# A cross-read with a GELU layer on one core: one sum, two bank copies and the state's transposes change places

## The chip, the cores and the metric

The kernel runs on one core of a Trainium2 chip. TensorE multiplies, VectorE and ScalarE do elementwise work and are the only ones that empty PSUM here, GpSimd (POOL) copies between SBUF tiles and issues loads, SyncE (SP) issues the stores and the transposing DMAs. Each engine works through its own queue strictly in order. The metric is the device time of one launch in microseconds; three runs of the kernel before gave a median of 205.29 us (205.24 to 205.36).

## The reference

`x` is 8 batches by 8 heads by 512 rows of 64 numbers, `state` the same with 32 rows instead of 512. For every batch and head:

```python
a = softmax(x @ state.T / 8);   xread = a @ state      # 512 rows read the state
a2 = softmax(state @ x.T / 8);  sread = a2 @ x         # 32 rows read x
rows = concatenate(xread, sread)                        # 544 rows per batch and head
out = gelu(rows_of_all_heads(512) @ w_in) @ w_out       # 512 -> 2048 -> 512
```

The heads of a row are laid side by side (8 x 64 = 512 columns), so the second part works on 8 x 544 = 4352 rows.

## The kernel before, in words

**Staging.** A batch's 512 rows of x are one *turn* b; the 256 state rows of all batches are collected in `XSR` and put through both weights during the last turn. The work on `xread` is folded: for each batch `P = blockdiag(state) @ w_in` (256 by 2048, `p_mm`, lines 423 to 436, in four *chunks* of 512 columns, each with two PSUM banks t = 0 and 1) takes the place of `w_in`, so that a hidden chunk is `gelu(P.T @ a.T)`: `M` (lines 489 to 501) makes hidden chunk m of 128 columns with two matmuls of 512 columns (`hp`), and ScalarE's Gelu (line 501) writes `g`. Sixteen chunks make a batch.

**The second product.** `g @ w_out` is computed per batch as a 2 x 2 block product with seven block products in place of eight, `X(b, name)` (line 621) with names 3, 4, 5, 1, 2, 7, 6: 16 matmuls each, into four fixed PSUM banks `o0` to `o3` (3 and 5 share `o0`, 4 and 2 `o1`, 1 and 7 `o2`, 6 has `o3`). Five of them need a sum of two quadrants of `g`, which VectorE makes just ahead: `g_sum(b, name)` (line 582, 128 x 2048 bf16, tile `gsum`, three buffers). Sum "6" is quadrant (1, 0) minus (0, 0), so it needs the hidden chunks 0 to 7; sum "5" needs all sixteen. Results are combined on VectorE (lines 618, 640, 652, 654) and GpSimd (lines 610, 646), and stored by SP (line 605). Line 618 is the output addition behind product "2", which first needs GpSimd's `v`; line 654 is the one behind product "7", which empties bank `o2`.

**The loop.** Turn 0 and most of turn 1 are a separate run-up. The loop at line 1153 runs b = 2 to 7, each over eight *block pairs* p = 0 to 7; each pair makes two hidden chunks of batch b (`M(k, k + 1)`) and, mostly, one block product. For b < 7 and nb = b + 1:

- p = 0: sum 5 and product 4 of batch b - 1, sum 1; a load of x and its re-layout on GpSimd (`rearr`, line 225). For b = 2 also chunk 2 of P of batch 2 (`pmat(2, 2)`)
- p = 1: scores and Exp of batch nb; product 5, sum 2
- p = 2, 3: the two halves of the normalization of batch nb (`norm`, lines 353 to 356); product 1 and sum 7 in p = 2; in p = 3 sum "6" of batch b, product 2 of batch b - 1, and for b = 2 also chunk 3 of P (`pmat(2, 3)`)
- p = 4: two hidden chunks alone
- p = 5: the transposing DMA of a (`atr_dma`, SP's queue); product 7 of batch b - 1; then `p_all`; `rearr_ones` on GpSimd (line 235); product 3 of batch b
- p = 6: two hidden chunks (12 and 13)
- p = 7: `srt(b)`, hidden chunks 14 and 15, product 6 of batch b

**p_all** (line 929) first does the state's read of batch b (`reads_mm`: matmuls of line 905 into one PSUM tile, copied out by ScalarE in line 913 as `sraw`), then the four chunks of P for batch nb, then the eight bank copies (`p_copy`: ScalarE t = 0, VectorE t = 1), then `reads_norm` on VectorE (lines 921, 922), which leaves the normalized read `srm`. In turn 6 it reads batches 6 and 7 together. The eight banks of P come from the fixed `o0`, `o1`, `o3`, `o2` (chunk 0 bank 0, chunk 2 banks 0 and 1, chunk 3 bank 0) and from a pool of four rotating banks `f` (the other four), which `hp`, the state's read and the transposes `srT` share. So the fourth chunk needs line 654 to have emptied `o2`, product 3 needs ScalarE's copy out of `o0`, and product 6 needs `o3` and sum "6".

**srt** (line 413) transposes `srm` on TensorE into a tile of the pool `f` and has VectorE copy it into `XSR`, where the batch is the innermost index (a stride of eight numbers). In turn 6 it is called twice, with two tiles.

The order on every queue is the order of these calls: the tile framework runs with a manual schedule and adds only the semaphores.

Of the kernel before, what the change touches and what calls it, by code (L numbers as in the profile page):

```python
# [10 lines left out]
BF16 = mybir.dt.bfloat16  # L11
# [6 lines left out]
def kernel(  # L18
# [8 lines left out]
    nc = tc.nc  # L27

    B, H, S, D = x.shape
    _, _, NS, _ = state.shape  # L30
# [3 lines left out]
    HC = H // 2  # L34
# [33 lines left out]
    ident = persist.tile([128, 128], BF16, name="ident")  # L68
# [161 lines left out]
    def rearr_ones(b):  # L230
        A = atts[b]
        eng = nc.vector if b < 2 else nc.gpsimd
        src = xbs[b].rearrange("p (t c) (j d) -> p t c j d", t=2, d=D)
        for t in range(2):
            eng.tensor_copy(  # L235
                out=A.xo[:, :, :, 2 + 64 * t:66 + 64 * t].rearrange("p j c d -> p c j d"),
                in_=src[:, t],
            )
# [174 lines left out]
    def srt(b):  # L413
        A = atts[b]
        ps = ps_f.tile([128, HC, NS], BF16, name="srT", tag="f")
        nc.tensor.transpose(  # L416
            ps.rearrange("p c n -> p (c n)"), A.srm.rearrange("q t d -> q (t d)"), ident
        )
        nc.vector.tensor_copy(out=XSR[:, :, :, b], in_=ps)  # L419

    Ps = {}

    def p_mm(b, f, tiles):
        if b not in Ps:
            Ps[b] = att.tile([128, 2, d_ff], BF16, name="P", tag="P")
        ps = [tiles([128, 512], "p_ps") for t in range(2)]
        for c in range(HC):
            for t in range(2):
                nc.tensor.matmul(  # L429
                    ps[t][32 * c:32 * c + 32, :],  # L430
                    lhsT=sbd[64 * t:64 * t + 64, b, c, 32 * t:32 * t + 32],
                    rhs=w_in_bf[64 * t:64 * t + 64, c, f * 512:(f + 1) * 512],
                    start=True,
                    stop=True,
                )
        return ps

    def p_copy(b, f, ps):
        dst = Ps[b][:, :, f * 512:(f + 1) * 512]
        nc.scalar.copy(out=dst[:, 0, :], in_=ps[0])  # L440
        nc.vector.tensor_copy(out=dst[:, 1, :], in_=ps[1])  # L441

    def pmat(b, f):
        p_copy(b, f, p_mm(b, f, ftile))
# [137 lines left out]
    def g_sum(b, name):  # L582
        (h0, k0), (h1, k1), op = G_SUMS[name]
        t = apool.tile([128, MH, 256], BF16, name="gsum", tag="gsum")
        nc.vector.tensor_tensor(out=t, in0=g_q(b, h0, k0), in1=g_q(b, h1, k1), op=op)  # L585
        xs[b, "g" + name] = t
# [34 lines left out]
    def X(b, name):  # L621
        bank = {"3": 0, "4": 1, "5": 0, "2": 1, "1": 2, "6": 3, "7": 2}[name]
        first = name in "3416"
        if first:
            xs[b, bank] = otile([128, 2, NH], "xp", bank)
        ps = xs[b, bank]
        lhs = {"3": (0, 0), "4": (1, 1)}.get(name)
        lhs = xs[b, "g" + name] if lhs is None else g_q(b, *lhs)
        rhs = {"5": w_q[1][1], "2": w_q[0][0]}.get(name)
        rhs = w_sum[name] if rhs is None else rhs  # L630
        x_mm(ps, lhs, rhs, first)
        if name == "3":
            xs[b, "s3"] = c_tile("s3")
            if b > 1:
                nc.scalar.copy(out=xs[b, "s3"], in_=ps)
            for h in range(2):
                xs[b, "o", h] = hpool.tile([128, 2, d_model], FP32, name="oh", tag=f"oh{h}")
        elif name == "4":
            xs[b, "s34"] = c_tile("s34")
            nc.vector.tensor_tensor(out=xs[b, "s34"], in0=ps, in1=xs[b, "s3"], op=ALU.add)  # L640
        elif name == "5":
            o = xs[b, "o", 0][:, :, NH:]
            nc.scalar.copy(out=o, in_=ps)  # L643
            xs[b, "u"] = c_tile("u")
            x_out(b, 0, right)
            nc.gpsimd.tensor_tensor(out=xs[b, "u"], in0=xs[b, "s34"], in1=o, op=ALU.subtract)  # L646
        elif name == "2":
            nc.scalar.copy(out=xs[b, "o", 1][:, :, :NH], in_=ps)  # L648
            c22(b)
        elif name == "1":  # L650
            xs[b, "q"] = c_tile("q")
            nc.vector.tensor_tensor(out=xs[b, "q"], in0=ps, in1=xs[b, "s34"], op=ALU.add)  # L652
        elif name == "7":
            nc.vector.tensor_tensor(  # L654
                out=xs[b, "o", 0][:, :, :NH], in0=ps, in1=xs[b, "u"], op=ALU.add
            )
            x_out(b, 0, left)
# [258 lines left out]
    def reads_norm(bs, raw):  # L916
        for i, b in enumerate(bs):
            A = atts[b]
            A.srm = att.tile([128, 2, D], BF16, name="srm", tag="srm")
            inv = att.tile([128, 2], FP32, name="inv", tag="inv")  # L920
            nc.vector.reciprocal(out=inv, in_=raw[:, i, 0:130:129])
            nc.vector.tensor_tensor(
                out=A.srm,
                in0=raw[:, i, 1:129].rearrange("q (t d) -> q t d", t=2),
                in1=inv[:, :].to_broadcast((128, 2, D)),
                op=ALU.mult,
            )

    def p_all(b, bs):
        raw = reads_mm(bs)  # L930
        done = []
        for f, at in enumerate(((0, None), (None, None), (1, 3), (2, None))):
            it = iter(at)

            def tiles(shape, name):
                i = next(it)
                return ftile(shape, name) if i is None else otile(shape, name, i)

            done.append((b, f, p_mm(b, f, tiles)))
        for x in done:  # L940
            p_copy(*x)
        reads_norm(bs, raw)

    def p_copy_v(b, f, ps):
        for t in range(2):
# [207 lines left out]
    for b in range(2, B):  # L1153
        nb = b + 1
        for p in range(8):
            k = 16 * b + 2 * p
            if p == 1 and nb < B:
                scores(nb, 0)
                scores(nb, 1)
            if p in (2, 3) and nb < B:  # L1160
                norm(nb, p - 2)
            if p == 3 and nb + 1 < B:
                xtr_dma(nb + 1)
            if p == 5 and nb < B:
                atr_dma(nb)
            if p == 7 and nb < B:
                srt(b)
                if nb == B - 1:
                    srt(nb)
            if nb == B and p < 5:  # L1170
                read_out_slot(p)
                if p == 4:
                    r_homes()
                    r_sum("5")
                    r_sum("2")
                continue
            M(k, k + 1)
            if b == 2 and p in (0, 3):
                pmat(2, 2 + p // 3)
            if b == 2 and p == 1:  # L1180
                w_sums(4)
            if p < 4 or (p == 4 and nb == B):
                if p == 0:
                    g_sum(b - 1, "5")
                    if b > 2:
                        sr_w("5216"[b - 3])
                if p == 3:
                    g_sum(b, "6")
                X(b - 1, "45127"[p])
                if p < 3:  # L1190
                    g_sum(b - 1, "127"[p])
            if p == 0 and b + 3 < B:
                hold_for(b, 0)
                load_x(4 if b == 2 else b + 3)
            if p == 6 and b == 2:
                hold_for(b, 12)
                load_x(5)
            if p == 0 and nb + 1 < B:
                begin(nb + 1)
                rearr(nb + 1)  # L1200
            if nb == B:
                if p == 5:
                    g_sum(b, "6")
                    R("3")
                    r_sum("1")
                    R("4")
                    r_sum("6")
                    r_sum("7")
                if p == 6:
                    R("5")  # L1210
                    X(b, "3")
                    R("2")
                    R("1")
                if p == 7:
                    R("6")
                    X(b, "6")
                continue
            if p == 5:
                X(b - 1, "7")
                reads = (b, nb) if nb == B - 1 else (b,)  # L1220
                p_all(nb, reads)
                if b == 2:
                    rearr_ones(3)
                elif nb + 1 < B:
                    rearr_ones(nb + 1)
                X(b, "3")
            if p == 7:
                if b == 2:
                    rearr_ones(4)
                X(b, "6")  # L1230
    b = B - 1
    for name in "521":
# [39 lines left out]
```

## Time and profile before

| what | us |
|---|---|
| median of three runs | 205.29 |
| profiled execution | 205.13 |
| its span | 203.2 |
| TensorE busy (matmuls) | 196.0 (96%) |
| VectorE busy | 162.9 (80%) |
| ScalarE busy | 136.6 (67%) |
| GpSimd busy | 68.4 (34%) |
| sums `gsum` on VectorE, 35 | 50.2, mean 1.449, median 1.218, longest 3.166 |
| bank copies of P by line 441 on VectorE, 29 | 18.3, mean 0.681 |
| bank copies of P by line 440 on ScalarE, 29 | 15.3, mean 0.597 |
| copies into `XSR`, 8 | 5.7, mean 0.758 |
| granted TensorE clock | full throughout |

A line of the timeline reads: start, duration, engine, line of the kernel, operation, tile written and tiles read, shapes, number of instructions merged, and in brackets how long the engine stood idle before it and what released it. Durations of neighbours on one engine overlap by up to a tenth of a microsecond, so a row of four copies of 0.67 takes 2.48. PE is TensorE, PEld its weight loads, DVE VectorE, ACT ScalarE. Matmuls are pipelined: a busy TensorE need not be one at its peak, so lost time on it is read from the distance between the starts of two matmuls against the usual one (0.22 us for a matmul of 512 columns).

### The profile page before, as it was taken

To read this page: it belongs to the slowest core of one execution; us is meant where nothing else is said; L and a number is where in the kernel's file an instruction comes from. 1 tells how busy PE (TensorE), PEld (TensorE's weight loads), DVE (VectorE), ACT (ScalarE), POOL (GpSimd) and SP (SyncE) were. 2 spreads that over 40 slices of the span, in tenths; PEclk is the share of its full clock that TensorE was granted. 3 is DMA by queue.
4 is the path that set the end of the run, shared out by engine and by line. 5 is a ranking of instruction groups with operands and counts; after the bars stand their busy time and mean duration, and the time that the engine had idled before them with its cause. 6 is when DMAs were issued, how large, how long until landed. Compare 5 with 4: busy or idle time off the path is not lost.

```text
span 203.2 us, 4901 instructions
## 1 busy us (share of the span) xinstructions
PE 196.0 (96%) x2030; PEld 133.9 (66%) x2035; DVE 162.9 (80%) x255; ACT 136.6 (67%) x245; POOL 68.4 (34%) x75
## 2 busy tenths in 40 slices
PE   7899999999999999999999999999999999999993
PEld 2434544466766687666776677677776887878893
DVE  2954876789999889996899777967799888895882
ACT  3785678798985779656967597687857576864120
POOL 8972503324259297430527302420220002200000
PEclk9999999999999999999999999999999999999999
DMA  6999999986655879633772508270107001040134
GB/s 192 199 172 203 206 198 197 185 163 126 89 104 106 206 87 143 135 126 84 94 167 77 133 0 127 39 205 0 52 3 206 3 0 55 0 158 0 52 107 155
DMA packets 40566, 23.16 MB, mean 114 GB/s; under 512 B 21856, under 2 KB 39136, under 8 KB 40544
## 3 DMA queue, kind: packets, MB, share of 16 engines
q0 software_dynamic: 13984, 8.10, 29.3%
q1 hardware_dynamic: 25872, 14.36, 27.7%
q10 hardware_dynamic: 688, 0.39, 0.6%
q8 instruction: 16, 0.26, 0.5%
q14 instruction: 6, 0.05, 0.1%
HBM read 17.30 MB, written 8.91 MB: 129 GB/s over the span
## 4 chain that ended last, share of the span: by engine, by line
PE 68%; DVE 15%; DMA 5%; POOL 4%; issue 4%; ACT 2%; DVEq 0%; POOLq 0%; ACTq 0%
PE xp L591 30%; PE hp L494 20%; DVE gsum L585 6%; DMA xb<-in_x_dram 5%; PE op L536 3%; PE sp L798 3%; PE rp L864 3%; POOL w_in_bf L105 2%; DVE P L441 2%; DVE a L356 2%; PE op L520 2%; PE xp L703 2%; PE p_ps L429 2%; DVE cs L353 1%; PE pt L333 1%
## 5 line engine op out<-in xcount | busy, mean ns | idle before, releaser
L501 ACT ACTIVATE g<-hp 128x512 bf16<-128x512 f32 x124 | 66.3, 606 | 21.5 <-PE hp L494 17.0
L494 PE MATMUL hp<-AT,P 128*128 128x512 bf16 x248 | 62.0, 379 | 0.6 <-DVE P L441 0.4
L591 PEld LDWEIGHTS <-gsum 128*128 128x128 bf16 x528 | 51.4, 98 | 11.4 <-DVE q L652 0.2
L585 DVE TENSOR_TENSOR gsum<-g 128x2048 bf16<-128x2048 bf16 x35 | 50.2, 1449 | 4.1 <-ACT g L501 4.0
L494 PEld LDWEIGHTS <-P 128*128 128x128 bf16 x248 | 23.2, 98 | 21.1 <-issue 2.2
L591 PE MATMUL xp<-ws,gsum 128*128 128x256 bf16 x304 | 36.3, 273 | 0.0
L591 PE MATMUL xp<-ws,g 128*128 128x256 bf16 x224 | 26.8, 273 | 0.2
L591 PE MATMUL xp<-w_out_bf,gsum 128*128 128x256 bf16 x224 | 26.6, 273 | 0.0
L591 PEld LDWEIGHTS <-g 128*128 128x128 bf16 x224 | 21.5, 98 | 5.0 <-issue 1.6
L646 POOL TENSOR_TENSOR u<-s,oh 128x512 f32<-128x512 f32 x6 | 8.8, 1467 | 40.6 <-ACT oh L643 40.6
L225 POOL COPY x<-xb 128x1024 bf16<-128x1024 bf16 x12 | 14.3, 1225 | 16.6 <-DMA xb<-in_x_dram 16.6
L441 DVE CAST P<-p_ps 128x512 bf16<-128x512 f32 x29 | 18.3, 681 | 1.2 <-PE p_ps L429 1.0
L440 ACT CAST P<-p_ps 128x512 bf16<-128x512 f32 x29 | 15.3, 597 | 4.8 <-PE p_ps L429 4.7
L235 POOL COPY xo<-xb 128x1024 bf16<-128x1024 bf16 x12 | 13.2, 1129 | 5.0 <-PE sr L905 5.0
L610 POOL TENSOR_TENSOR v<-q,oh 128x512 f32<-128x512 f32 x6 | 8.2, 1371 | 19.6 <-ACT oh L648 17.2
L356 DVE TENSOR_TENSOR a<-e,ics 128x512 bf16<-128x512 bf16 x14 | 11.7, 833 | 0.5
L536 PE MATMUL op<-w_out_bf,g 128*128 128x512 bf16 x44 | 11.1, 380 | 0.5 <-issue 0.3
L353 DVE TENSOR_REDUCE cs<-e 128x16 f32<-128x512 bf16 x14 | 9.5, 677 | 0.7 <-ACT e L340 0.7
L429 PE MATMUL p_ps<-w_in_bf,sbd 64*32 64x512 bf16 x248 | 9.6, 381 | 0.3 <-DVE oh L654 0.3
L501 ACT ACT_TABLE_LOAD x7 | 9.0, 1283 | 0.1
L419 DVE COPY XSR<-srT 128x128 bf16<-128x128 bf16 x8 | 5.7, 758 | 3.8 <-PE srT L416 3.8
L536 PEld LDWEIGHTS <-g 128*128 128x128 bf16 x48 | 4.1, 97 | 5.9 <-issue 1.1
(137 smaller groups left out, 233.2 us busy)
## 6 DMA issues: line engine op xcount, KB each, us to landing
out_dram<-oh SPq DMA_DIRECT2D x15, 256.0 KB, 2.7
xb<-in_x_dram POOLq DMA_DIRECT2D x7, 512.0 KB, 7.5
out_dram<-oh SPq DMA_DIRECT2D x6, 512.0 KB, 2.8
w_in_bf<-in_moe_w_in_dram POOLq DMA_DIRECT2D x6, 256.0 KB, 11.8
out_dram<-osb SPq DMA_DIRECT2D x5, 256.0 KB, 3.2
w_out_bf<-in_moe_w_out_dram POOLq DMA_DIRECT2D x4, 256.0 KB, 8.0
w_out_bf<-in_moe_w_out_dram POOLq DMA_DIRECT2D x2, 512.0 KB, 13.3
x0f<-in_x_dram SPq DMA_DIRECT2D x3, 256.0 KB, 3.8
```

The lines of the kernel that those rows point to most:

```text
L225: nc.gpsimd.tensor_copy(out=A.x4[:, :, :, 64 * t:64 * t + 64].rearrange("p j c d -> p c j d"), in_=src[:, t],)
L235: eng.tensor_copy(out=A.xo[:, :, :, 2 + 64 * t:66 + 64 * t].rearrange("p j c d -> p c j d"), in_=src[:, t],)
L353: nc.vector.reduce_sum(out=cs, in_=e4, axis=AX.X)
L356: nc.vector.tensor_tensor(out=A.a[:, :, hs].rearrange("p g (c n) -> p g c n", n=NS), in0=e4, in1=ics[:, :, :].to_broadcast((128, G, 2, NS) ...
L429: nc.tensor.matmul(ps[t][32 * c:32 * c + 32, :], lhsT=sbd[64 * t:64 * t + 64, b, c, 32 * t:32 * t + 32], rhs=w_in_bf[64 * t:64 * t + 64, c ...
L440: nc.scalar.copy(out=dst[:, 0, :], in_=ps[0])
L441: nc.vector.tensor_copy(out=dst[:, 1, :], in_=ps[1])
L494: nc.tensor.matmul(hp, lhsT=Ps[b][:, t, m * 128:(m + 1) * 128], rhs=atts[b].AT[:, :, t, :], start=(t == 0), stop=(t == 1),)
L501: nc.scalar.activation(out=gs[b][:, m, :], in_=hp, func=AF.Gelu)
L536: nc.tensor.matmul(ops[b, j], lhsT=gs[b][:, m, j * 128:(j + 1) * 128], rhs=w_out_bf[:, m, :], start=(m == 0), stop=(m == MC - 1),)
L585: nc.vector.tensor_tensor(out=t, in0=g_q(b, h0, k0), in1=g_q(b, h1, k1), op=op)
L591: nc.tensor.matmul(ps[:, j - js[0], :], lhsT=lhs[:, m, 128 * j:128 * j + 128], rhs=rhs[:, m, :], start=(first and j == js[0] and m == 0), ...
```

## The change

Three edits, all inside turns 2 to 6:

- Sum "6" of batch b leaves block pair 3 and is made behind `p_all` in block pair 5, so it stands on VectorE's queue behind the bank copies and `reads_norm`, and no longer ahead of lines 618 and 654.
- In `p_all` ScalarE copies both banks of chunk 0 (five copies instead of four; VectorE three instead of four). In turn 2, block pair 3, ScalarE copies both banks of chunk 3 of batch 2.
- The transposes of `srm` stand behind hidden chunks 14 and 15 instead of ahead of them, and those of turn 6 share one PSUM tile and leave it in one VectorE copy.

The queues of GpSimd and SP keep their order.

```diff
+    def srts(bs):
+        ps = ps_f.tile([128, len(bs), HC, NS], BF16, name="srT", tag="f")
+        for i, b in enumerate(bs):
+            nc.tensor.transpose(
+                ps[:, i].rearrange("p c n -> p (c n)"),
+                atts[b].srm.rearrange("q t d -> q (t d)"),
+                ident,
+            )
+        nc.vector.tensor_copy(
+            out=XSR[:, :, :, bs[0]:bs[-1] + 1], in_=ps.rearrange("p b c n -> p c n b")
+        )
...
     def p_all(b, bs):
...
-        for x in done:
-            p_copy(*x)
+        for b, f, ps in done:
+            for t in range(2):
+                copy = nc.scalar.copy if t == 0 or f == 0 else nc.vector.tensor_copy
+                copy(out=Ps[b][:, t, f * 512:(f + 1) * 512], in_=ps[t])
         reads_norm(bs, raw)
+
+    def p_copy_s(b, f, ps):
+        for t in range(2):
+            nc.scalar.copy(out=Ps[b][:, t, f * 512:(f + 1) * 512], in_=ps[t])
...
-            if p == 7 and nb < B:
-                srt(b)
-                if nb == B - 1:
-                    srt(nb)
...
             M(k, k + 1)
-            if b == 2 and p in (0, 3):
-                pmat(2, 2 + p // 3)
+            if b == 2 and p == 0:
+                pmat(2, 2)
+            if b == 2 and p == 3:
+                p_copy_s(2, 3, p_mm(2, 3, ftile))
...
-                if p == 3:
-                    g_sum(b, "6")
                 X(b - 1, "45127"[p])
...
             if p == 5:
                 X(b - 1, "7")
                 reads = (b, nb) if nb == B - 1 else (b,)
                 p_all(nb, reads)
+                g_sum(b, "6")
...
             if p == 7:
                 if b == 2:
                     rearr_ones(4)
+                srts(reads)
                 X(b, "6")
```

More of the change, by code (lines that the diff above doesn't have):

```diff
@@ L927, in reads_norm, with p_all @@
             )
-    def p_all(b, bs):
+    def p_all(nb, bs):
         raw = reads_mm(bs)
@@ L937, in tiles @@
                 return ftile(shape, name) if i is None else otile(shape, name, i)
-            done.append((b, f, p_mm(b, f, tiles)))
-        for x in done:
-            p_copy(*x)
+            done.append((nb, f, p_mm(nb, f, tiles)))
+        for b, f, ps in done:
+            for t in range(2):
+                copy = nc.scalar.copy if t == 0 or f == 0 else nc.vector.tensor_copy
+                copy(out=Ps[b][:, t, f * 512:(f + 1) * 512], in_=ps[t])
         reads_norm(bs, raw)
+    def p_copy_s(b, f, ps):
+        for t in range(2):
+            nc.scalar.copy(out=Ps[b][:, t, f * 512:(f + 1) * 512], in_=ps[t])
     def p_copy_v(b, f, ps):
```

## The prediction

> **What bounds the kernel now.** I read the chain that ended last, then busy time by turn of the loop, then TensorE's own timeline for the places where it stood still, then VectorE and GpSimd side by side at those places. The chain's shares:
>
> ```profile
> PE 68%; DVE 15%; DMA 5%; POOL 4%; issue 4%; ACT 2%; DVEq 0%; POOLq 0%; ACTq 0%
> ```
>
> In order of time its VectorE part lies in three stretches, 51.67 to 63.8, 72.4 to 88.9 and 106.9 to 113.7 us (turns 2, 3 and 4). From 113.7 to 200.1 us it runs through TensorE but for about 3 us in all. So VectorE's time counts in turns 2 to 4 and is nearly worthless later. The stretches below are turns 2 to 6, from one block pair 0 to the next:
>
> ```profile
> 50.20:72.97 22.77, 22.26 (x244) 15.38 (x242) 20.47 (x28) 16.87 (x30) 11.98 (x12) 1.00 0.61 119
> 72.97:94.65 21.68, 21.49 (x227) 15.26 (x225) 20.03 (x25) 15.79 (x28) 11.52 (x10) 1.00 0.75 135
> 94.65:116.39 21.74, 21.48 (x227) 15.23 (x225) 19.33 (x25) 15.90 (x28) 10.14 (x10) 1.00 0.53 110
> 116.39:137.64 21.25, 21.20 (x227) 15.36 (x225) 17.14 (x25) 15.79 (x28) 4.69 (x4) 1.00 0.43 89
> 137.64:159.67 22.03, 21.80 (x260) 15.69 (x258) 18.92 (x30) 15.95 (x28) 2.65 (x2) 1.00 0.20 61
> ```
>
> (length, then busy time of TensorE, weight loads, VectorE, ScalarE, GpSimd, then granted clock.) Turn 5, 21.25 us, is what a turn lasts when TensorE never waits: turns 3 and 4 hold the same matmuls and last 0.43 and 0.49 longer, with VectorE at 20.0 and 19.3 us of 21.7. ScalarE has 5 to 6 us free in each. TensorE's timeline shows where the excess lies:
>
> ```profile
> 63.87 0.59 PE L494 MATMUL hp<-AT,P 128*128 128x512 bf16 x2 [0.40 <-DVE P L441]
> ...
> 87.80 0.99 PE L429 MATMUL p_ps<-w_in_bf,sbd 64*32 64x512 bf16 x24
> 88.99 0.41 PE L429 MATMUL p_ps<-w_in_bf,sbd 64*32 64x512 bf16 x8 [0.19 <-DVE oh L654]
> 89.33 1.92 PE L591 MATMUL xp<-ws,g 128*128 128x256 bf16 x16
> ...
> 110.48 0.41 PE L429 MATMUL p_ps<-w_in_bf,sbd 64*32 64x512 bf16 x8 [0.15 <-DVE oh L654]
> 110.82 1.92 PE L591 MATMUL xp<-ws,g 128*128 128x256 bf16 x16
> 112.58 1.03 PE L494 MATMUL hp<-AT,P 128*128 128x512 bf16 x4
> 113.72 0.23 PE L416 MATMUL srT<-ident,srm 128*128 128x128 bf16 x1
> ```
>
> ```profile
> 131.22 1.06 PE L429 MATMUL p_ps<-w_in_bf,sbd 64*32 64x512 bf16 x32
> 132.33 1.91 PE L591 MATMUL xp<-ws,g 128*128 128x256 bf16 x16
> ...
> 156.46 0.36 PE L416 MATMUL srT<-ident,srm 128*128 128x128 bf16 x2
> 156.99 1.10 PE L494 MATMUL hp<-AT,P 128*128 128x512 bf16 x4 [0.17 <-ACT g L501]
> 157.93 1.91 PE L591 MATMUL xp<-ws,gsum 128*128 128x256 bf16 x16
> ```
>
> **The change, part by part.** Times are of the profiled run, 205.13 us with a span of 203.2, 0.16 under the median of 205.29.
>
> (1) Turn 2, block pair 3: the second bank of chunk 3 goes from VectorE to ScalarE. VectorE takes it at 63.14, behind two sums and a normalization; the bank is wanted for the hidden chunk of 63.87. That matmul starts 0.78 after its predecessor's start at 63.08, against 0.22 in the row's usual step: 0.57 lost. ScalarE frees the first bank at 61.14 and then idles 1.06, so the second is free by about 61.7, 1.4 before it is wanted: minus 0.57. Its next work, the copy at 62.20, waits for matmuls and keeps its place. Bounds: 0 and 0.57; I take all of it, since weights and sums of the next product are ready (sum 7 ends 61.53).
>
> (2) Block pair 3: the sum "6" leaves VectorE's queue ahead of the two output additions (lines 618, 654). In turn 3 it ran 86.52 to 87.73, so line 654, ready when product "7" ends (about 87.5), ran at 88.26 and held the fourth chunk's bank. First chunk to product "3" took 1.53 us there (87.80 to 89.33), 1.34 in turn 4 (109.48 to 110.82), 1.11 in turn 5. With the sum gone line 654 ends near 88.2, ahead of the fourth chunk's own 88.45: minus 0.42 and minus 0.23. Behind the sum also stood SP's output write and, after it, the transpose of a: they leave sooner. GpSimd's v, which the first addition needs, ends at 86.05 and 108.15, in time.
>
> (3) The copies. ScalarE's fifth lasts about 0.5 (four take 2.05); product "3"'s copy follows 0.58 after its fourth (turn 5: 134.33), 0.8 to 1.0 in turns 3 and 4, so it moves by nothing or a few hundredths. Product "3" itself waits for the first bank, still copied first. VectorE does three instead of four: minus 0.6, but its first now waits for chunk 1, whose matmuls start 0.2 later.
>
> (4) The sum's new place: after the normalization, 1.21 us if nothing shares its way, and product "6" waits for it. Turn 6's first VectorE copy, released by TensorE, came 0.50 after its chunk's first matmul; by that, copies start at 131.95 in turn 5, the normalization ends 134.2, the sum 135.4; product "6" starts at 135.90. Spare: 0.5, and likewise 0.5 in turns 2 and 3 (70.6 against 71.2; 91.9 against 92.5) and 0.2 in turn 6 (157.3 against 157.5, two normalizations). No cost in four turns. Turn 4 is different:
>
> ```profile
> 109.52 2.03 POOL L235 COPY xo<-xb 128x1024 bf16<-128x1024 bf16 x2 [1.38 <-PE sr L905]
> 111.49 2.03 POOL L225 COPY x<-xb 128x1024 bf16<-128x1024 bf16 x2
> ```
>
> ```profile
> 98.07 3.74 DVE L585 TENSOR_TENSOR gsum<-g 128x2048 bf16<-128x2048 bf16 x2
> ...
> 106.93 2.29 DVE L585 TENSOR_TENSOR gsum<-g 128x2048 bf16<-128x2048 bf16 x1
> ...
> 112.92 0.74 DVE L922 TENSOR_TENSOR srm<-sraw,inv 128x128 bf16<-128x128 f32 x1
> ...
> 134.32 0.29 DVE L922 TENSOR_TENSOR srm<-sraw,inv 128x128 bf16<-128x128 f32 x1
> ```
>
> Only there do four GpSimd copies run on end to 113.52. The normalization's product takes 0.74 instead of 0.29 and ends with them; sums that meet GpSimd take about 2.3 (106.93) or wait out both copies (98.07, beside 97.57 to 99.59). In the new order the product comes up at 112.2, is held to 113.66 all the same, and the sum ends 114.8, the product "6" starts at 114.9. Without waits it would start at 114.64 minus 0.23 minus the 0.27 that the transpose lost at 113.72, so at 114.14: a new wait of 0.76. Net of the whole turn: plus 0.26. Bounds: minus 0.50 (the sum slips in) to plus 0.9 (held as long as the longest row, 3.17).
>
> [...]
>
> (5) The transposes one pair later: same number, 0.06 each, now between hidden chunk 15 and product "6". Turn 4 no longer waits there for the normalization (counted). In turn 6 the two PSUM tiles made chunk 14 wait for a Gelu: 0.34 at 156.59 to 156.99 and 0.08 after it; in the new order chunk 14 takes a bank that VectorE has emptied: minus 0.42 (bounds 0.34 and 0.49, all three excesses there). The transposes of one turn 6 tile leave in one copy: between 0.73 (one row) and 1.37 (two); by the larger it ends near 159.1, the differences for the state's product by 159.6, 0.5 before TensorE wants them (160.53 less 0.4). In turns 2 to 5 the copy moves to just before sum "5", which waits 0.8 to 1.0 for Gelu 15: hidden.
>
> Sum: 0.57 + 0.42 - 0.26 + 0.42 = 1.15 off 205.13 = 203.98; on the median 204.15.
>
> **The rivals.** *A, no wait in turn 4*: the sum gets between GpSimd's copies as at 78.3 us, where a sum ran between two of them. Sum 1.91: 203.4. Against it: there the first copy had itself been held. *B, part is given back*: VectorE has no idle time from 72.2 to 88.9, so 0.57 won in turn 2 may meet a late sum in turn 3, or product "6" waits 0.5 in one further turn: about 204.7. Against: sum "5" and GpSimd's copies there hang on Gelus of the same turn 2, which move along. *C, slower*: the sum takes its collisions along. Three of the five old ones took 2.29 to 2.31 instead of 1.21, beside GpSimd's v. At 2.3 the new sum ends 0.6 late in turns 2, 3 and 5, 0.9 in turn 6, 0.76 in turn 4: 3.5 against 1.91 won, 206.9. It decides once those waits pass 1.91 + 0.41, with the sum at some 2.0 us on average. Against: v (128.21, 149.46) stands at the old place, and at the new one GpSimd is idle after 133.3 in turn 5 and throughout in turn 6. *D, nothing*: ScalarE's fifth copy and one or two small waits take back what was won: 205.2.
>
> **How the numbers follow.** Main case 0.50, A 0.13, B 0.14, D 0.09, C 0.14. A measurement can tell about 0.2%, 0.41 us, from no change. Main, A and B lie below 204.88: faster 0.77; D same 0.09; C slower 0.14. The range runs from 203.2 (A with turn 6 at its upper bound and slack in the sums) to 205.4 (D with a tenth's spread), leaving out C. The main case alone: 203.8 to 204.5.
>
> **What would show it.** Turn 2: no VectorE wait of the hidden chunks after block pair 4. Turns 3 and 4: first chunk to product "3" near 1.11 us, with line 654 at product "7"'s end. Sum "6" at 1.21 us behind the normalization except in turn 4, where TensorE stands before product "6" for some 0.8. Turn 6: chunk 14 right behind chunk 13. Turn 5 stays 21.25. The prediction is wrong if weight loads of product "6" wait for VectorE in other turns, or if the Gelus of chunks 12 to 15 start later because ScalarE's fifth copy holds the copy of product "3".

## The result, and the profile after

The changed kernel takes 203.44 us (median of five runs, 203.34 to 203.97) against 205.29 (five runs, 205.05 to 206.0) beside it: a ratio of 0.9913, 95% interval 0.9892 to 0.9935. It is faster, by 1.85 us there; measured twice more it was faster by 1.56 (203.81 against 205.37) and 1.20 (204.02 against 205.22). The profiled execution took 203.97 us with a span of 202.1.

The chain that ended last, by engine:

```profile
PE 91%; DVE 5%; ACT 2%; issue 1%; ACTq 0%
```

VectorE's share went from 15% to 5%; 4.4 us of it (2% of the span) lie in one place of turn 4, shown below. The same stretches as before, turns 2 to 6 from one block pair 0 to the next (length, then busy time of TensorE, weight loads, VectorE, ScalarE, GpSimd, granted clock):

```profile
50.15:72.31 22.16, 22.05 (x244) 15.40 (x242) 18.91 (x26) 17.75 (x32) 10.98 (x12) 1.00 0.61 122
72.31:93.52 21.21, 21.16 (x227) 15.37 (x225) 19.58 (x24) 16.28 (x29) 11.76 (x10) 1.00 0.87 138
93.52:115.33 21.81, 21.34 (x227) 15.33 (x225) 18.77 (x25) 16.28 (x29) 10.22 (x10) 1.00 0.53 110
115.33:136.54 21.21, 21.16 (x227) 15.37 (x225) 15.19 (x23) 16.28 (x29) 4.67 (x4) 1.00 0.45 89
136.54:158.08 21.54, 21.48 (x260) 15.70 (x258) 16.26 (x28) 16.31 (x29) 2.65 (x2) 1.00 0.23 62
```

Turn 2 fell from 22.77 to 22.16, turn 3 from 21.68 to 21.21, turn 6 from 22.03 to 21.54. Turn 3 now equals turn 5. Turn 4 alone did not fall (21.74, now 21.81). TensorE's timeline of the changed kernel at the places shown before:

```profile
61.94 1.89 PE L506 MATMUL hp<-AT,P 128*128 128x512 bf16 x8
...
87.14 1.06 PE L441 MATMUL p_ps<-w_in_bf,sbd 64*32 64x512 bf16 x32
88.25 1.91 PE L603 MATMUL xp<-ws,g 128*128 128x256 bf16 x16
...
112.93 0.22 PE L424 MATMUL srT<-ident,srm 128*128 128x128 bf16 x1
113.57 1.92 PE L603 MATMUL xp<-ws,gsum 128*128 128x256 bf16 x16 [0.42 <-DVE gsum L597]
...
154.50 1.89 PE L506 MATMUL hp<-AT,P 128*128 128x512 bf16 x8
156.22 0.28 PE L424 MATMUL srT<-ident,srm 128*128 128x128 bf16 x2
156.34 1.91 PE L603 MATMUL xp<-ws,gsum 128*128 128x256 bf16 x16
```

The hidden chunks of turn 2 run through (eight matmuls in one row); first chunk to product "3" takes 1.11 us in turn 3 as in turn 5; the four hidden chunks around the old place of the transposes of turn 6 run through too. The one wait left by the change is new: 0.64 from the transpose to product "6" in turn 4, where turn 3 needs 0.06. What VectorE does there:

```profile
109.08 1.89 DVE L955 CAST P<-p_ps 128x512 bf16<-128x512 f32 x3 [0.28 <-PE p_ps L441]
110.88 0.15 DVE L933 RECIPROCAL inv<-sraw 128x2 f32<-128x2 f32 x1
111.07 0.47 DVE L934 TENSOR_TENSOR srm<-sraw,inv 128x128 bf16<-128x128 f32 x1
111.47 2.05 DVE L597 TENSOR_TENSOR gsum<-g 128x2048 bf16<-128x2048 bf16 x1
```

and GpSimd beside it:

```profile
108.39 2.03 POOL L235 COPY xo<-xb 128x1024 bf16<-128x1024 bf16 x2 [1.38 <-PE sr L917]
110.36 2.08 POOL L225 COPY x<-xb 128x1024 bf16<-128x1024 bf16 x2
```

The last of the four copies ends at 112.44; the sum takes 2.05 instead of about 1.22 (turn 3: 90.06, 1.22) and ends 1.08 after it.

### The profile page after: what moved, and what is told of

The parts are those of the page before. It is cut to its first block, busy times and chain, and to the rows that moved or that the text cites. A ratio compares the mean times of both kernels' runs of the same rounds, so it can differ in the third digit from the quotient of the medians.

```text
span 202.1 us, 4900 instructions
## 1 busy us (share of the span) xinstructions
PE 195.0 (97%) x2030; PEld 134.4 (66%) x2035; DVE 155.9 (77%) x248; ACT 139.2 (69%) x251; POOL 67.3 (33%) x75
## 4 chain that ended last, share of the span: by engine, by line
PE 91%; DVE 5%; ACT 2%; issue 1%; ACTq 0%
PE xp L603 40%; PE hp L506 26%; PE op L548 5%; PE sp L810 3%; PE rp L876 3%; PE p_ps L441 2%; PE op L532 2%; PE xp L715 2%; PE pt L333 2%; PE warm_ps L150 2%; PE sr L917 1%; ACT P L955 1%; DVE gsum L597 1%; DVE P L955 1%; PE hp L1064 1%
## 5 line engine op out<-in xcount | busy, mean ns | idle before, releaser
L506 PE MATMUL hp<-AT,P 128*128 128x512 bf16 x248 | 61.2, 379 | 0.0
L597 DVE TENSOR_TENSOR gsum<-g 128x2048 bf16<-128x2048 bf16 x35 | 47.3, 1367 | 0.5
L235 POOL COPY xo<-xb 128x1024 bf16<-128x1024 bf16 x12 | 12.1, 1041 | 5.0 <-PE sr L917 5.0
L955 ACT CAST P<-p_ps 128x512 bf16<-128x512 f32 x25 | 12.7, 606 | 0.1
L955 DVE CAST P<-p_ps 128x512 bf16<-128x512 f32 x15 | 9.4, 684 | 1.7 <-PE p_ps L441 1.7
```

The lines of the kernel that those rows point to most:

```text
L235: eng.tensor_copy(out=A.xo[:, :, :, 2 + 64 * t:66 + 64 * t].rearrange("p j c d -> p c j d"), in_=src[:, t],)
L506: nc.tensor.matmul(hp, lhsT=Ps[b][:, t, m * 128:(m + 1) * 128], rhs=atts[b].AT[:, :, t, :], start=(t == 0), stop=(t == 1),)
L955: copy(out=Ps[b][:, t, f * 512:(f + 1) * 512], in_=ps[t])
```

## The experiments

Each timed run stood beside runs of the kernel before on the same chip. The medians of one kernel differ from one measurement to the next by up to 0.6 us (the changed kernel: 203.44, 203.81, 204.02), so a few tenths are read from the traces: the distance on TensorE's timeline from the first hidden chunk of one turn to that of the next, in us. Every kernel's turn 7 to TensorE's end lasts 40.44.

| kernel | turn 2 | turn 3 | turn 4 | turn 5 | turn 6 | median |
|---|---|---|---|---|---|---|
| before | 22.76 | 21.68 | 21.74 | 21.25 | 22.03 | 205.29 |
| changed | 22.16 | 21.22 | 21.81 | 21.21 | 21.54 | 203.44 |
| changed, second profile | 22.16 | 21.22 | 21.81 | 21.21 | 21.54 | 203.81 |
| changed, third profile | 22.16 | 21.22 | 21.81 | 21.22 | 21.54 | 204.02 |
| turn 2's bank back | 22.57 | 21.21 | 21.81 | 21.21 | 21.54 | 204.96 |
| the same again | 22.76 | 21.21 | 21.81 | 21.22 | 21.54 | 204.63 |
| sum back | 22.16 | 21.64 | 21.46 | 21.22 | 21.54 | 203.98 |
| transposes back | 22.20 | 21.25 | 21.81 | 21.25 | 22.50 | 204.94 |
| fifth copy back | 22.16 | 21.21 | 21.95 | 21.21 | 21.84 | 204.05 |
| before, sum alone moved | 22.64 | 21.25 | 21.95 | 21.25 | 22.88 | 205.42 |
| copies twice in turn 5 | 22.16 | 21.22 | 21.81 | 21.81 | 21.54 | 204.49 |
| x of batch 7 held | 22.16 | 21.22 | 21.21 | 21.21 | 21.54 | 202.90 |
| the same again | 22.16 | 21.22 | 21.21 | 21.21 | 21.54 | 202.95 |

**Turn 2's bank back on VectorE.**

```diff
-                p_copy_s(2, 3, p_mm(2, 3, ftile))
+                pmat(2, 3)
```

> The changed kernel, but turn 2's second bank of chunk 3 is copied by VectorE again. Theory (each part is worth the wait it removes): the hidden chunk of turn 2's block pair 5 waits again for VectorE, 0.57 us between two matmul starts, and nothing else moves: 203.44 + 0.57 = 204.0. Rival (VectorE is the bound of turns 2 and 3, so its work counts, not its order): one copy of 0.6 us more on VectorE would show in turn 3 too, and the loss is 0.6 to 1.2.

Measured: 204.96 us, ratio 0.9983 (0.9966 to 1.0001). The wait is back:

```profile
63.53 1.46 PE L506 MATMUL hp<-AT,P 128*128 128x512 bf16 x6
65.24 0.59 PE L506 MATMUL hp<-AT,P 128*128 128x512 bf16 x2 [0.25 <-DVE P L453]
```

Turn 2 lost 0.41 and no other turn moved, against the rival; the median lost more than that, and this profile's first sum came some 1.6 us later than in the others (47.88 against 45.9 to 46.5). So it was run again beside the changed kernel:

> Turn 2's bank on VectorE again, once more: its first median, 204.96, lies 0.8 above what its turns explain (0.41 in turn 2, nothing else), and its profile had a run-up 1.7 us longer than the others. Theory (the turns tell the cost; the rest is the run-up's scatter): 0.4 above the changed kernel of the same call. Rival (the edit also makes the run-up longer): again 1.1 to 1.5 above it, with the first sum of the profile after 47 us instead of 46.2.

Measured: 204.63 against 204.02 of the changed kernel beside it, ratio to before 0.9959 (0.9939 to 0.9979). Turn 2 lost 0.60, nothing else, and the first sum came at 46.34. The longer run-up did not come back, so it is put down to scatter. TensorE's wait in this profile:

```profile
63.89 0.59 PE L506 MATMUL hp<-AT,P 128*128 128x512 bf16 x2 [0.44 <-DVE P L453]
```

The edit costs 0.4 to 0.6, and the 0.60 of this trace is all that turn 2 had won. The difference between the two runs fits one row: the first half of the normalization (line 356), ahead of the bank copy on VectorE's queue, lasted 0.87 us in the first run and 1.05 in the second (1.02 in the kernel before, from 58.54, beside GpSimd's copies of x of 57.98 to 60.46; 0.69 in its turns 5 and 6, where GpSimd copied no x beside it).

**The sum back in block pair 3.**

```diff
+                if p == 3:
+                    g_sum(b, "6")
                 X(b - 1, "45127"[p])
...
                 p_all(nb, reads)
-                g_sum(b, "6")
```

> The changed kernel, but sum 6 stands in block pair 3 again. Theory: turn 3 loses 0.42 and turn 4 0.23 before product 3, as before, because line 654 comes late again; turn 4 wins back the 0.59 that TensorE now waits for the sum before product 6. Net plus 0.06: 203.5, though turn by turn both signs show. Rival (moving the sum is what made the kernel faster): 0.7 or more slower, 204.1 and up. Second rival (the bank copies did it all): no turn changes.

Measured: 203.98, ratio 0.9927 (0.9906 to 0.9949). The turns show both signs: turn 3 plus 0.42, turn 4 minus 0.35, net 0.08. In turn 4 the old wait before product "3" and no new one before product "6":

```profile
109.62 0.41 PE L441 MATMUL p_ps<-w_in_bf,sbd 64*32 64x512 bf16 x8 [0.15 <-DVE oh L666]
109.96 1.92 PE L603 MATMUL xp<-ws,g 128*128 128x256 bf16 x16
111.72 1.89 PE L506 MATMUL hp<-AT,P 128*128 128x512 bf16 x8
113.45 0.22 PE L424 MATMUL srT<-ident,srm 128*128 128x128 bf16 x1
113.50 1.91 PE L603 MATMUL xp<-ws,gsum 128*128 128x256 bf16 x16
```

So the move of the sum, the most visible part of the change, is worth next to nothing here, beside the other two edits: it takes 0.42 in turn 3 and gives nearly all of it back in turn 4. By the turns both rivals fall; the median, 203.98, lies close to the first rival's 204.1 and could not tell.

**The transposes back ahead of hidden chunks 14 and 15**, in two tiles in turn 6.

```diff
+            if p == 7 and nb < B:
+                srt(b)
+                if nb == B - 1:
+                    srt(nb)
...
-                srts(reads)
```

> The changed kernel, but the state's transposes stand ahead of hidden chunks 14 and 15 again, in two tiles in turn 6. Theory: turn 6 loses 0.49 us (chunk 14 waits for a Gelu), the other turns nothing: 203.9. Rival (the pool's rotation does not matter, turn 6 won by its bank copies): no loss, 203.4.

Measured: 204.94, ratio 0.9978 (0.9958 to 0.9998); turn 6 lost 0.96, twice what was expected, the others 0.04 at most. TensorE in turn 6:

```profile
155.83 0.59 PE L506 MATMUL hp<-AT,P 128*128 128x512 bf16 x2 [0.25 <-ACT g L513]
156.81 0.59 PE L506 MATMUL hp<-AT,P 128*128 128x512 bf16 x2 [0.39 <-DVE XSR L419]
```

The first row is the expected wait for a Gelu. The second is one that the kernel before did not have: `XSR` is copied behind sum "6" on VectorE's queue now, so the two transposes hold two banks of the pool until the sum is done (156.13 here; the two copies follow from 156.04, 1.28 in all), and by the releaser that the row names chunk 15 wants one of them. Moving the sum and moving the transposes belong together, and the expectation had treated them as independent.

**The fifth copy back to VectorE.**

```diff
-                copy = nc.scalar.copy if t == 0 or f == 0 else nc.vector.tensor_copy
+                copy = nc.scalar.copy if t == 0 else nc.vector.tensor_copy
```

> The changed kernel, but VectorE copies the second bank of chunk 0 again (four copies each). Theory: the normalization and sum 6 end 0.4 later; the spare of 0.5 in turns 2, 3 and 5 covers it, turn 6 (spare 0.15) loses about 0.25, turn 4 nothing, since its sum waits for GpSimd anyhow: plus 0.25 to 0.4, 203.7 to 203.85. Rival (the fifth copy is what lets the sum move at all): the loss is 0.4 in each of five turns, 205.4.

Measured: 204.05 against 203.81 of the changed kernel beside it, ratio to before 0.9941 (0.9920 to 0.9961). Turn 6 lost 0.30 and turn 4 0.14; turns 2, 3 and 5 nothing, so the spare of 0.5 there was real and the rival (0.4 in each of five) falls. Turn 4 was not expected to move: the normalization of the state's read came up some 0.4 us later (3.35 after line 666's start at 107.97, instead of 2.97 after 108.10) and took 1.07 instead of 0.47. By an estimate GpSimd's fourth copy ran from 111.21 to 112.31 there (111.34 to 112.44 in the changed kernel, less the 0.13 by which line 666 starts earlier), so the normalization would have come up just behind that copy's start and waited it out. VectorE in turn 4 of this kernel:

```profile
111.14 0.15 DVE L933 RECIPROCAL inv<-sraw 128x2 f32<-128x2 f32 x1
111.32 1.07 DVE L934 TENSOR_TENSOR srm<-sraw,inv 128x128 bf16<-128x128 f32 x1
112.31 1.21 DVE L597 TENSOR_TENSOR gsum<-g 128x2048 bf16<-128x2048 bf16 x1
```

**The kernel before with the sum alone moved.**

```diff
-                if p == 3:
-                    g_sum(b, "6")
...
                 p_all(nb, reads)
+                g_sum(b, "6")
```

> The kernel before, with only sum 6 moved behind the bank copies. Theory: turn 3 wins 0.42, turn 4 wins 0.23 before product 3 and loses 0.2 to 0.7 before product 6, turn 2 keeps its 0.57 and turn 6 its 0.49: 204.7 to 205.3. Rival (the sum's move carries the change): 203.9 or less.

Measured: 205.42, ratio 1.0007 (0.9993 to 1.0022). Turn 3 won 0.43, turn 4 lost 0.21, as expected; turn 2 won 0.12 and turn 6 lost 0.85, which were not. Turn 2 still has its wait for VectorE's bank copy, shorter by as much as the normalization's row ahead of that copy (0.90 us instead of 1.02). Turn 6 by its TensorE row:

```profile
157.56 0.59 PE L494 MATMUL hp<-AT,P 128*128 128x512 bf16 x2 [0.77 <-DVE XSR L419]
```

It is the wait that the run with the transposes back showed. By the turns, the sum moved alone costs 0.51 us; the median, 205.42 against 205.37 of the kernel before beside it, shows no change. Either way it gains nothing; its companions are what make the change.

**GpSimd's copies of turn 5 done twice**, so that four stand in a row there too.

```diff
                 elif nb + 1 < B:
                     rearr_ones(nb + 1)
+                    if b == 5:
+                        rearr_ones(nb + 1)
```

> The changed kernel, with GpSimd's two ones copies of turn 5 done twice in a row, so that four copies follow each other there as they do in turn 4. Theory (a run of four GpSimd copies behind the state's read holds up sum 6): turn 5 shows what turn 4 shows, a sum of about 2 us and 0.6 between the transpose and product 6, plus 0.6: 204.0. Rival (turn 4's wait is its own, from another source): no change, 203.4.

Measured: 204.49 against 203.81 of the changed kernel beside it, ratio to before 0.9960 (0.9942 to 0.9979). Turn 5 grew from 21.21 to 21.81, turn 4's length to the hundredth. GpSimd's four copies, then TensorE's wait, then VectorE, which in turn 5 of this kernel repeats turn 4 of the changed one:

```profile
130.10 4.05 POOL L235 COPY xo<-xb 128x1024 bf16<-128x1024 bf16 x4 [1.79 <-PE sr L917]
```

```profile
135.28 1.92 PE L603 MATMUL xp<-ws,gsum 128*128 128x256 bf16 x16 [0.42 <-DVE gsum L597]
```

```profile
132.77 0.47 DVE L934 TENSOR_TENSOR srm<-sraw,inv 128x128 bf16<-128x128 f32 x1
133.17 2.05 DVE L597 TENSOR_TENSOR gsum<-g 128x2048 bf16<-128x2048 bf16 x1
```

**The re-layout of x for batch 7 held back**, by a one-element copy on GpSimd that reads turn 5's first hidden chunk.

```diff
             if p == 0 and nb + 1 < B:
+                if b == 5:
+                    hold_for(b, 0)
                 begin(nb + 1)
                 rearr(nb + 1)
```

> The changed kernel, with GpSimd's re-layout of x for batch 7 held back until turn 5's first hidden chunk has gone through its Gelu, so it no longer runs behind the ones copies of turn 4. Theory (those two copies hold up sum 6 of turn 4): the sum takes 1.21 instead of 1.99 us, TensorE's 0.59 before product 6 of turn 4 is gone, 202.85. Rival (the copies then hold up sums 1 and 2 of turn 5 just as long): a new wait ahead of product 1 in turn 5, up to 1.0, and no gain: 203.4 to 203.9.

Measured: 202.90 (202.63 to 203.74), ratio 0.9882 (0.9860 to 0.9905). Turn 4 is 21.21, the length of turn 5. GpSimd, then VectorE, then TensorE's product "6":

```profile
108.52 2.03 POOL L235 COPY xo<-xb 128x1024 bf16<-128x1024 bf16 x2 [1.38 <-PE sr L917]
116.27 0.39 POOL L967 COPY hold<-g 128x1 bf16<-128x1 bf16 x1 [5.72 <-ACT g L513]
116.59 2.02 POOL L225 COPY x<-xb 128x1024 bf16<-128x1024 bf16 x2
```

```profile
111.41 1.22 DVE L597 TENSOR_TENSOR gsum<-g 128x2048 bf16<-128x2048 bf16 x1
118.28 2.54 DVE L597 TENSOR_TENSOR gsum<-g 128x2048 bf16<-128x2048 bf16 x2
```

```profile
113.12 1.91 PE L603 MATMUL xp<-ws,gsum 128*128 128x256 bf16 x16
```

The two copies moved to 116.6; sum "6" takes 1.22 and ends at 112.6, half a microsecond ahead of product "6" (113.12). The rival's new wait is absent: sums "1" and "2" of the next turn, 2.54 us together instead of 2.35, pay some 0.2 us to the copies, which end at 118.6, and nothing waits for them. Once more beside the changed kernel:

> The held re-layout of x for batch 7, once more beside the changed kernel on one chip. Theory: 0.6 below it, all of it in turn 4 (21.21 instead of 21.81). Rival (its first median was a lucky chip): no difference.

Measured: 202.95 against 204.02, ratio to before 0.9883 (0.9849 to 0.9917). The turns explain 0.60 of that difference; the rest is not explained by any turn. This is the fastest version of the study, both times. Here the sum's move does pay: turns 3 and 4 are 21.22 and 21.21, against 21.64 and 21.46 with the sum back in block pair 3 and the copies not held. The sum back with the copies held was not run.

**The changed kernel again, twice.**

> The changed kernel once more, for a second profile. The first profiled execution lasted 203.97 with a span of 202.1, the four others 203.3 to 203.5 with spans of 201.4 to 201.6. Theory (its last stores landed late): TensorE's last product ends at the same 198.5 as in the first profile, and the last store lands 2.0 instead of 2.4 us after its issue, span about 201.6. Rival (turn 4's wait is shorter in most executions): TensorE ends some 0.4 earlier and the distance before product 6 of turn 4 is near the normal.

> The changed kernel a third time, beside the two below on one chip, since medians of one kernel have differed by 0.4 us between calls. Turns 2 to 6 as in both profiles so far (22.16, 21.22, 21.81, 21.21, 21.54); median 203.4 to 203.8.

Measured: 203.81 (twelve runs, 202.94 to 205.52; ratio 0.9930, 0.9908 to 0.9953) and 204.02 (seven runs, 203.39 to 204.39; ratio 0.9930, 0.9899 to 0.9961). Turns 2 to 6 repeat to 0.01 us in all three profiles, so turn 4's wait is there each time and the rival falls. From TensorE's end to the end of the span it is 3.55, 3.66 and 2.94 us, 3.12 in the profile before; so the last stores and what follows them scatter by 0.7. The theory's span of 201.6 was not met by the second profile (202.1); the third has 201.7. There is no trace of the unprofiled executions, so whether those with spans of 201.4 us had a shorter end is not shown.

## Why the prediction was right, and where it was off

The forecast was faster, 204.15 in 203.2 to 205.4; 203.44 was measured, and 203.8 to 204.0 the two times after it. The turns add up to 0.60 + 0.46 - 0.07 + 0.04 + 0.49 = 1.52 where the sum of the terms said 1.15.

- *Term (1), turn 2, 0.57*: measured 0.60, and the run that undid it alone gave 0.60 back the second time. Right. It is a matter of order: on ScalarE the bank was free at 61.57, well before it was wanted (63.24, the seventh matmul of the row of 61.94), while VectorE came to it at 63.14 in the kernel before, behind two sums and a normalization.
- *Term (2), 0.42 and 0.23*: right, to the hundredth. Line 666 (the old 654) follows product "7" at once (in turn 4 the product ends at 108.06 and the line starts at 108.10), and first chunk to product "3" takes 1.11 in every turn but turn 2, which has 1.17 before and 1.16 after.
- *Term (3)*: ScalarE's fifth copy cost nothing. Right. VectorE's first copy waits 0.28 for chunk 1, as said.
- *Term (4), the sum's new place*: no cost in turns 2, 3, 5 and 6, right; the run with the fifth copy back confirms that turns 2, 3 and 5 had room and turn 6 nearly none. Turn 4's new wait was named, in its place and from its cause, and the runs that remove and reproduce the row of copies show that cause. Its size was 0.76 by the forecast and 0.58 beyond the usual step by the trace. The step that was off is that the normalization is held to the end of the fourth copy: it slipped in after the third (0.47 us instead of 0.74), and the sum ended 1.08 after the fourth, where the forecast had 1.28 (114.8 against 113.52). Net of the turn: plus 0.07, not plus 0.26.
- *Term (5), turn 6, 0.42*: measured 0.49, the upper bound; all three excesses went, not two. In turns 2, 3 and 5 the move also saved 0.04 each, by the run that undid it, which was not counted; so turn 5's 21.25 was not quite the length of a turn without waits. The merged copy into `XSR`, bounded by 0.73 and 1.37 (the two rows of the kernel before lasted 1.30 in all), took 0.42, below both ends.

What the terms missed by, 0.37 us, is turn 4 (0.19), turn 6 (0.07), turn 3 (0.04), turn 5 (0.04) and turn 2 (0.03). The other 0.3 to the first median is within the scatter of the medians: the changed kernel was 1.85, 1.56 and 1.20 below the kernel before, 1.54 on average.

The parts do not add up one by one. Undone alone, they cost 0.60 (turn 2's bank), 0.08 (the sum), 1.08 (the transposes) and 0.44 (the fifth copy) by the turns, 2.20 in all against 1.52 won: the transposes and the fifth copy also pay for waits that only the moved sum brings.

Rival A, "no wait in turn 4", was priced at 203.4, the time that was measured first. It is wrong all the same: the wait is there in three profiles, and the run that really takes it away lands at 202.9. The time alone would have picked the wrong case. Rival B did not occur: sum "5" of turn 2's batch started 0.62 earlier (72.24, now 71.62), about as much as TensorE ran ahead (turn 3 began 0.66 earlier), and turn 3 won in full. Rival C's mechanism, the sum meeting GpSimd at its new place, exists in one turn out of five; the run that copies twice in turn 5 shows its price, 0.60 a turn, so by that price, as an estimate, five such turns would have cost 3.0 against some 2.1 won elsewhere (the 1.52 and turn 4's 0.60).

## What to carry to other kernels

Where TensorE is the bound in most of the time and VectorE in some turns, look for what waits behind a long VectorE instruction in its queue, not for VectorE's total: in turn 5 VectorE is busy for 1.95 us less, and the turn gained 0.04 us. When an instruction moves, look at what now stands behind it and holds a buffer (here the transposes' PSUM banks), and at what runs on another engine beside it in the new place (here GpSimd's copies, with which the sum took 2.05 us instead of 1.22); one block in five may be different, and that one decides whether the move pays. Then read the gain turn by turn, since two opposite effects can add up to a time that fits the wrong story.

## What was not expected of the hardware

- Copying the transposed state out of PSUM took less time for two batches at once than for one. In the trace after, 128 x 256 numbers with the two batches adjacent took 0.424 us, 128 x 128 with single numbers 16 bytes apart 0.73 us:

```profile
L419 DVE COPY XSR<-srT x2: 731/732/734, 21.9 to 33.5; 128x128 bf16<-128x128 bf16 x2
L429 DVE COPY XSR<-srT x5: 424/729/748, 70.8 to 156.5; 128x128 bf16<-128x128 bf16 x4, 128x256 bf16<-128x256 bf16 x1
```

```profile
156.54 0.42 DVE L429 COPY XSR<-srT 128x256 bf16<-128x256 bf16 x1 [0.35 <-PE srT L424]
```

  (In the first two lines: smallest, median and largest duration in ns.) The two copies differ in their size and in their stride, and no run here changed the stride alone: what makes the pair the faster one was not shown.
- Who goes first where VectorE and GpSimd meet. In turn 4 of the changed kernel the normalization, whose row starts at 111.07 while the third copy ran (110.36 to 111.40), went ahead of the fourth, which starts at 111.34 (it ended at 111.54, the fourth at 112.44), and the sum behind it, which starts at 111.47, waited for the fourth (it ended 1.08 after it): there the one that started earlier went first. With the fifth copy back on VectorE the normalization starts at 111.32, after the start of the fourth copy by the estimate above (111.21), and took 1.07, by the same order. But in the kernel before, the sum that starts at 98.07 took 2.61 and ended 1.09 after the second of two copies (97.57 to 98.62 and 98.55 to 99.59), which had started half a microsecond later than the sum. What decides between the two was not settled.
